# Soft-MoE attention on one core: the order of the last weight steps, and the cut of the output into stores

## The chip, the cores and the metric

One core of a Trainium2 chip runs the whole program. The metric is the device time of one execution in microseconds; the median of 3 runs is 369.21 us (368.94 to 369.48). Engines: PE (TensorE), DVE (VectorE), ACT (ScalarE), POOL (GpSimd) and SP (SyncE), which issues all the transfers that matter here, on one queue.

## The reference

An attention with sigmoid in place of softmax (8 batches, 12 heads, 448 rows, 64 columns) gives x of 3584 x 768. A soft mixture of 8 experts with 4 slots each follows:

```python
logits = x @ phi                                   # 3584 x 32
d = softmax of logits over the 3584 rows;  slot_input = d.T @ x
for e in range(8):                                 # w1: 768 x 1024, w2: 1024 x 768, float32
    slot_out[e] = np.maximum(slot_input[e] @ w1[e], 0.0) @ w2[e]
c = softmax of logits over the 32 slots
return c @ slot_out                                # 3584 x 768, 11 MB
```

## The kernel before

The first stage (to about 285 us) computes attention, logits and slot inputs, and loads the first weights beside it. Then come the w1 steps, and then w2 in two halves of 384 columns: for each half 16 steps n = 2e + g, where step n does experts e = n // 2 and half g of its 1024 hidden rows. A step (`w2_step`, matmul on L804) is four chunks `fl` on four column groups of PE, each float32 matmul two instructions, so 8 in the profile. POOL's copy on L800 puts the expert's 4 slots into `hw[e % 2]` once for each e and half.

Weights come in units of 384 KB; a step takes two. The loads go through SP's queue in the order of use (`load`, L169), as buffers come free; the last two of those are the halves of one load into `wpe`, for steps 13 and 14 of the second half. Step 15's weights are apart: unit `units[N_SEQ + 1]` (chunks 2 and 3) is put into `lt` by `load_kept`; of unit `units[N_SEQ]` the left half (chunk 0) lies in `wk`, loaded early by `load_wk`, and the right half (chunk 1, 192 KB) is loaded into `wpx` by `load_rest` (L137), which runs when no other load is left.

The output has 28 row blocks of 128 rows. `out_tile` (L750, L751) is one matmul of combine weights with the slot outputs of a half (`sts[hf]`) and a copy out of PSUM, on ACT for even and on DVE for odd tiles. Three kinds of stores take the tiles: `out_half` (L757) two row blocks of one half of the columns, 384 KB in pieces of 1536 bytes; `out_rows` (L764) one whole row block, 384 KB in pieces of 3072 bytes; `out_many` (L771) n whole row blocks, in pieces of n times 3072 bytes.

While the second half's steps run, `out_half` stores the first half's columns of row blocks 0 to `NH` - 1, a pair after each of the steps n = 4, 5, and so on. After step 15 the sum is gathered (`gather`, L777, ACT) and spread (`spread_sum`: two matmuls on L788, ACT on L790, DVE on L791), then the whole-row stores go out (`NR` = 2 of one block, then `MANY`), and at the end the second half's columns of blocks 0 to `NH` - 1. The order on PE, ACT, DVE and SP is that of the program.

Of the kernel before, what the change touches and what calls it, by code (L numbers as in the profile page):

```python
# [17 lines left out]
DM, NSLOT, E, SPE, F = 768, 32, 8, 4, 1024  # L18
# [34 lines left out]
FW = (NFC + 1) * NSLOT  # L53
ROWS = 128
NG = B * S // ROWS
NH = 16
LAG_T = 3
C4W = NBK * 4 * NSLOT
NR = 2
MANY = (2, 4, 4)  # L60
GROUPS = ((0, 1), (2, 3), (4, 5), (6,), (7,))
NB2 = 2 * NBK - 1
MANUAL = {mybir.EngineType.PE, mybir.EngineType.SP, mybir.EngineType.DVE, mybir.EngineType.Activation}
# [3 lines left out]
def soft_moe_attention(ctx: ExitStack, tc: tile.TileContext, qk, v, vl, phi, w, wq, w8, wz, cst, out):  # L67
# [71 lines left out]
    def w2_chunk(hf, e, g, fl):  # L139
        k = ("w2", hf, e, g, fl // 2)  # L140
        if k == units[N_SEQ] and fl % 2 == 0:
            return state["wh"]
        return utile[k][:, fl % 2 * HALF:(fl % 2 + 1) * HALF]
# [518 lines left out]
    def av_tile(name):  # L662
        turn[name] += 1
        return ps_av.tile([P, 512], F32, name=f"{name}{turn[name] % 2}")
# [53 lines left out]
    def combine_split(n):  # L718
        lt, k = pieces[n][:2]
        c4 = wc_last[:, n % 3 * C4W:(n % 3 + 1) * C4W].rearrange("p (k a z s) -> p k a z s", k=NBK, a=2, z=2)  # L720
        nc.vector.tensor_copy(c4[:, 0:k, 0, 0, :], lt)
        nc.vector.tensor_tensor(
            out=c4[:, 0:k, 0, 1, :], in0=lt, in1=c4[:, 0:k, 0, 0, :].bitcast(F32), op=ALU.subtract)
        nc.scalar.copy(c4[:, 0:k, 1, :, :], c4[:, 0:k, 0, :, :].bitcast(F32))
        return c4

    def combine_turn(n, c4):
        pt = pt_tile()
        _, k, t0, nt = pieces[n]
        for c in range(k):  # L730
            w = min(P, nt - c * P)
            nc.tensor.transpose(
                out=pt[:, c * P:c * P + w], in_=c4[0:w, c].rearrange("p a z s -> p (a z s)").bitcast(F32),
                identity=csb[0:w, 0:w])
        at0 = t0
        while at0 < t0 + nt:
            i, m = divmod(at0, UNIT)
            w = min(UNIT - m, t0 + nt - at0)
            if m == 0:
                cts[i] = state["wpb"].tile([P, UNIT], F32R, name=f"wc{i + 1}")[:]  # L740
            nc.scalar.copy(cts[i][:, m:m + w], pt[:, at0 - t0:at0 - t0 + w])
            at0 += w
# [10 lines left out]
    def out_half(m, hf):  # L753
        ov = ring_tile().rearrange("p (j c) -> p j c", j=2)
        for j in range(2):
            out_tile(ov[:, j, :], m + j, hf, j)
        nc.sync.dma_start(  # L757
            out[m * ROWS:(m + 2) * ROWS, hf * HALF:(hf + 1) * HALF].rearrange("(j p) c -> p j c", p=P), ov)

    def out_rows(m):  # L760
        ov = ring_tile().rearrange("p (j c) -> p j c", j=2)
        for hf in range(2):
            out_tile(ov[:, hf, :], m, hf, hf)
        nc.sync.dma_start(out[m * ROWS:(m + 1) * ROWS, :].rearrange("p (j c) -> p j c", j=2), ov)  # L764

    def out_many(m, n):
        ov = ring_tile(n)
        for k in range(2 * n):
            t, hf = divmod(k, 2)
            out_tile(ov[:, k * HALF:(k + 1) * HALF], m, hf, hf, t, n)  # L770
        nc.sync.dma_start(out[m * ROWS:(m + n) * ROWS, :].rearrange("(p t) c -> p (t c)", t=n), ov)  # L771
# [3 lines left out]
    def gather(po):  # L775
        so = sb2.tile([P, HALF], F32, name="tmp")
        nc.scalar.copy(so[:], po[:, 0:HALF])  # L777
        return so

    def spread_sum(so, cuts=(0, HALF)):  # L780
        if sts:
            st = wc_last[:, 0:HALF]
        else:
            st = sb2.tile([P, HALF], F32R, name="st")[:]
        parts = list(zip(cuts, cuts[1:]))
        prs = [ps_t.tile([P, 512], F32, name="pt") if k else av_tile("av1") for k in range(len(parts))]
        for pr, (c0, c1) in zip(prs, parts):
            nc.tensor.matmul(pr[:, 0:c1 - c0], rep, so[:, c0:c1], start=True, stop=True)  # L788
        for pr, (c0, c1) in zip(prs, parts):
            (nc.scalar.copy if len(parts) > 1 else nc.vector.tensor_copy)(st[:, c0:c1], pr[:, 0:c1 - c0])  # L790
            nc.vector.tensor_tensor(  # L791
                out=st[64:128, c0:c1], in0=pr[64:128, 0:c1 - c0], in1=st[64:128, c0:c1].bitcast(F32), op=ALU.subtract)
        sts.append(st)

    def w2_step(po, hf, n):
        e, g = divmod(n, 2)
        h = hw[e % 2]
        if g == 0:
            o = NSLOT - SPE
            nc.gpsimd.tensor_copy(  # L800
                h[:, o:o + NFC * NSLOT].rearrange("p (f s) -> p f s", f=NFC)[:, :, 0:SPE], hc[:, e])
        for fl in range(4):
            k = (4 * g + fl) * NSLOT + NSLOT - SPE - SPE * e
            nc.tensor.matmul(  # L804
                po[32 * fl:32 * fl + 32, 0:HALF], h[:, k:k + NSLOT], w2_chunk(hf, e, g, fl),
                start=(n == 0), stop=(n == 2 * E - 1))

    prev = None
    for e in range(E):
# [9 lines left out]

    po = av_tile("av1")  # L820
    for e in range(E):
        w2_step(po, 0, 2 * e)
        w2_step(po, 0, 2 * e + 1)
        if e >= LAG_T:
            combine_turn(e - LAG_T, c4s[e - LAG_T])
        c4s[e] = combine_split(e)
    assert state["next"] == N_SEQ
    so = gather(po)
    po = av_tile("av1")
    for n in range(2 * E):  # L830
        w2_step(po, 1, n)
        if n == 1:
            spread_sum(so)
        if n < LAG_T:
            combine_turn(E - LAG_T + n, c4s[E - LAG_T + n])
            if n == LAG_T - 1:
                sctx.close()
                ps_t = ctx.enter_context(tc.tile_pool(name="ps_t", bufs=4, space=PSUM, reuse_waits="tile"))
        if 4 <= n < 4 + NH // 2:
            out_half(2 * (n - 4), 0)  # L840
    spread_sum(gather(po), (0, HALF // 2, HALF))
    for m in range(NH, NH + NR):
        out_rows(m)
    m = NH + NR
    for n in MANY:
        out_many(m, n)
        m += n
    assert m == NG
    for m in range(0, NH, 2):
        out_half(m, 1)  # L850
# [50 lines left out]
```

## Time and profile before

| | |
|---|---|
| median of 3 runs | 369.21 us (368.94 to 369.48) |
| the profiled execution | 369.13 us, of which the span of instructions is 367.4 us |
| mean granted clock | 0.982 |
| PE busy | 347.7 us (95%) |
| DVE, ACT, POOL busy | 242.4, 222.5, 9.1 us |
| read from and written to memory | 83.53 MB, 11.01 MB |

Shares of busy time are means over stages with different limits: PE is at 9 tenths or more in nearly all slices up to 280 us, while the DMA engines are at 9 tenths or more in the last quarter. Times below are us from the start of the span.

### The profile page before, as it was taken

The numbers are of one execution on the slowest core, as the hardware profiler recorded it, in microseconds if no ns is written. First come the engines' busy times: TensorE is split into PE (matmuls) and PEld (weight loads), VectorE is DVE, ScalarE is ACT, GpSimd is POOL, SyncE is SP. The second block draws the span as 40 slices with busy tenths as digits, with TensorE's granted clock in tenths as the row PEclk, the third lists the DMA queues.
The fourth block names the chain that finished last, engine by engine and source line by source line (L and its number), as shares of the span: only waits on it lengthen the run. The fifth ranks groups of instructions, "written<-read, shape, count | busy, mean of one in ns | idle before, by whom it ended". The sixth has DMA issues, their size and how long they took to land.

```text
span 367.4 us, 10340 instructions
## 1 busy us (share of the span) xinstructions
PE 347.7 (95%) x4309; PEld 159.6 (43%) x4309; DVE 242.4 (66%) x621; ACT 222.5 (61%) x306; POOL 9.1 (2%) x39
## 2 busy tenths in 40 slices
PE   9999999999999999999999999999999999799850
PEld 5333333544444346444434644464556553233620
DVE  0148829887795886959948696889875785123650
ACT  5777777667777773777777387748674114322640
POOL 1000000000000000000000000000003001000000
PEclk9999999999999999999999999999999999989995
DMA  6666675565676663666676377829899999999998
GB/s 218 218 208 205 204 222 186 183 204 163 231 222 211 199 198 114 210 199 202 204 227 184 128 249 251 290 62 366 286 308 363 435 421 430 416 423 405 403 417 300
DMA packets 34639, 95.21 MB, mean 259 GB/s; under 512 B 3616, under 2 KB 17568, under 8 KB 33312
## 3 DMA queue, kind: packets, MB, share of 16 engines
q1 hardware_dynamic: 34592, 94.55, 73.3%
q8 instruction: 34, 0.56, 0.6%
q14 instruction: 13, 0.11, 0.1%
HBM read 83.53 MB, written 11.01 MB: 257 GB/s over the span
## 4 chain that ended last, share of the span: by engine, by line
PE 81%; DMA 14%; DVE 1%; ACT 0%; issue 0%; ACTq 0%; SPq 0%
PE sc L274 35%; PE av L315 34%; DMA wpe<-in_wq_dram 9%; DMA wa<-in_w_dram 5%; PE sc L431 2%; PE sc L377 2%; PE av L187 2%; DVE wa L751 1%; PE av L750 1%; PE sc L359 1%; PE av L545 1%; PE av L290 1%; PE pt L750 1%; PE av L431 0%; PE av L804 0%
## 5 line engine op out<-in xcount | busy, mean ns | idle before, releaser
L282 ACT ACTIVATE att<-sc,sm 128x896 f32<-128x896 f32 x167 | 167.9, 1008 | 81.0 <-PE sc L274 77.8
L315 PE MATMUL av<-att,v 64*64 64x448 f32 x1128 | 131.1, 536 | 0.0
L274 PE MATMUL sc<-qk 64*64 64x448 f32 x896 | 111.7, 537 | 0.0
L315 PEld LDWEIGHTS av<-att,v 64*64 64x64 f32 x1128 | 42.5, 133 | 63.4 <-issue 63.0
L274 PE MATMUL sc<-wk 64*64 64x448 f32 x440 | 59.7, 551 | 0.0
L340 DVE STREAM_TRANSPOSE wa<-wpe 32x384 f32<-32x384 f32 (+5 forms) x144 | 58.0, 403 | 2.2
L274 PEld LDWEIGHTS sc<-qk 64*64 64x64 f32 x896 | 35.6, 133 | 49.7 <-issue 40.4
L340 DVE STREAM_TRANSPOSE wa<-xy 32x192 f32<-32x192 f32 (+3 forms) x96 | 33.1, 344 | 1.6
L322 DVE TENSOR_TENSOR wpe<-wpe,av 128x448 f32<-128x448 f32 x18 | 11.2, 621 | 32.0 <-PE av L315 20.8
L274 PEld LDWEIGHTS sc<-wk 64*64 64x64 f32 x440 | 18.4, 136 | 24.1 <-issue 20.5
L340 DVE STREAM_TRANSPOSE wa<-wpx 32x288 f32<-32x288 f32 (+1 forms) x48 | 24.9, 520 | 0.8
L804 PE MATMUL av<-wa,hw 128*32 128x384 f32 x208 | 20.9, 507 | 2.5 <-DMA wa<-in_w_dram 2.5
L322 DVE TENSOR_TENSOR wpx<-wpx,av 128x448 f32<-128x448 f32 x15 | 9.3, 621 | 19.7 <-PE av L315 17.4
L315 PE MATMUL av<-att,vl 64*64 64x448 f32 x188 | 22.3, 536 | 0.0
L187 PE MATMUL av<-wa,phi 128*32 128x256 f32 x312 | 17.6, 380 | 0.4 <-DVE phi L512 0.4
L322 DVE TENSOR_TENSOR xy<-xy,av 128x448 f32<-128x448 f32 x14 | 8.7, 621 | 8.0 <-ACT xy L318 4.0
L751 DVE COPY wa<-pt 128x384 f32<-128x384 f32 x23 | 11.9, 555 | 3.2 <-PE pt L750 2.8
L751 ACT COPY wa<-av 128x384 f32<-128x384 f32 x23 | 10.7, 481 | 4.6 <-PE av L750 4.0
L187 PEld LDWEIGHTS av<-wa,phi 128*32 128x32 f32 x312 | 9.7, 110 | 7.1 <-DVE tmp L694 0.9
L697 ACT COPY t<-tmp 128x32 f32<-128x32 f32 x8 | 1.7, 218 | 17.5 <-DVE tmp L695 17.5
L315 PEld LDWEIGHTS av<-att,vl 64*64 64x64 f32 x188 | 7.3, 133 | 10.8 <-issue 10.8
L340 DVE STREAM_TRANSPOSE wpe<-xy 32x256 f32<-32x256 f32 (+3 forms) x32 | 11.0, 344 | 0.5
(184 smaller groups left out, 285.6 us busy)
## 6 DMA issues: line engine op xcount, KB each, us to landing
wa<-in_w_dram SPq DMA_DIRECT2D x52, 384.0 KB, 4.1
qk<-in_qk_dram SPq DMA_DIRECT2D x32, 448.0 KB, 3.7
wa<-in_w_dram SPq DMA_DIRECT2D x4, 3072.0 KB, 19.4
v<-in_v_dram SPq DMA_DIRECT2D x48, 192.0 KB, 2.6
wk<-in_qk_dram SPq DMA_DIRECT2D x15, 448.0 KB, 3.4
wa<-in_wq_dram SPq DMA_DIRECT2D x4, 1536.0 KB, 32.5
out_dram<-wa SPq DMA_DIRECT2D x13, 384.0 KB, 7.4
out_dram<-wa SPq DMA_DIRECT2D x2, 1536.0 KB, 7.5
```

Of the source, the lines that this page charges most:

```text
L187: nc.tensor.matmul(ph[32 * j:32 * j + 32, 0:256], phi_sb[:, kc, :], wt, start=(kc == 0), stop=(kc == NKC - 1))
L274: nc.tensor.matmul(sc[h][64 * t:64 * t + 64, 0:S], qkts[pt][r, S + k0:S + k0 + 64], qkts[pt][r, 0:S], start=True, stop=True)
L282: nc.scalar.activation(att[:], tile2[:, :, 0:S], AF.Sigmoid, bias=nbias, scale=QSCALE)
L290: nc.tensor.matmul(o[k][r, 0:t.stop - t.start], w[:, r], att[:, h, t], start=start, stop=stop)
L315: nc.tensor.matmul(o[t][r, 0:S], w, att[row, h, :], start=start, stop=stop)
L322: nc.vector.tensor_tensor(out=x_of(p), in0=x_of(p), in1=av[0][:, 0:S], op=ALU.add)
L340: nc.vector.transpose(y[32 * g:32 * g + 32, k0:k0 + n, c0:c0 + m, BLK * a:BLK * a + BLK], src)
L377: nc.tensor.matmul(lg[32 * j:32 * j + 32, BLK * c0[j]:BLK * (c0[j] + n)], phi_sb[:, hp, :], blocks(x, j if x is xa else (j + 2) % 4, n), s ...
L431: nc.tensor.matmul(sls[t][32 * a:32 * a + 32, :], zt[:, c * BLK:(c + 1) * BLK], y_of(t, gi, c)[:, :, BLK * a:BLK * a + BLK], start=(c == 0 ...
L750: nc.tensor.matmul(pf[:, 0:HALF], ct_of(m, t, n), sts[hf], start=True, stop=True)
L751: (nc.scalar.copy, nc.vector.tensor_copy)[k % 2](ov, pf[:, 0:HALF])
L804: nc.tensor.matmul(po[32 * fl:32 * fl + 32, 0:HALF], h[:, k:k + NSLOT], w2_chunk(hf, e, g, fl), start=(n == 0), stop=(n == 2 * E - 1))
```

## The change

Three edits. Step 15 of the second half moves ahead of steps 13 and 14 (`ORDER2`); the first and last matmul of the sum are told by position, and the copy into `hw` is made when the pair (half, e) changes. `NH` is 14: seven stores by halves in each half, the last of the first half after n = 10. The whole rows are 14 blocks, stored by 1, 1, 2, 4, 2, 4.

```diff
-NH = 16
+NH = 14
-MANY = (2, 4, 4)
+MANY = (2, 4, 2, 4)
+ORDER2 = tuple(range(13)) + (15, 13, 14)
...
+    held_e = {}
+
-    def w2_step(po, hf, n):
+    def w2_step(po, hf, n, first, last):
         e, g = divmod(n, 2)
         h = hw[e % 2]
-        if g == 0:
+        if held_e.get(e % 2) != (hf, e):
+            held_e[e % 2] = hf, e
             o = NSLOT - SPE
             nc.gpsimd.tensor_copy(
...
-                start=(n == 0), stop=(n == 2 * E - 1))
+                start=first, stop=last)
...
-        w2_step(po, 0, 2 * e)
-        w2_step(po, 0, 2 * e + 1)
+        w2_step(po, 0, 2 * e, e == 0, False)
+        w2_step(po, 0, 2 * e + 1, False, e == E - 1)
...
-        w2_step(po, 1, n)
+        w2_step(po, 1, ORDER2[n], n == 0, n == 2 * E - 1)
```

PE around the last steps of the second half, before, right behind step 11 (`wa`: step 12, `wpe`: 13 and 14, `wk`, `wpx`, `lt`: 15; `hw_3401` is for e = 6, `hw_3402` for e = 7; a wait in brackets names a semaphore; DMAHW2, 3 and 4 are those of the two `wpe` loads and of `load_rest`):

```order
L750 MATMUL av_3980<-st,wc_3825 128x384 [waits Activation_49]
L750 MATMUL pt<-st,wc_3825 128x384 [waits DVE_49]
L804 MATMUL av_3849<-wa_3653,hw_3401 32x384 [waits Pool_49]
L804 MATMUL av_3849<-wa_3653,hw_3401 32x384 x3
L804 MATMUL av_3849<-wpe,hw_3401 32x384 [waits DMAHW2_49]
L804 MATMUL av_3849<-wpe,hw_3401 32x384 x3
L804 MATMUL av_3849<-wpe,hw_3402 32x384 [waits DMAHW3_49,Pool_49]
L804 MATMUL av_3849<-wpe,hw_3402 32x384 x3
L804 MATMUL av_3849<-wk,hw_3402 32x384
L804 MATMUL av_3849<-wpx,hw_3402 32x384 [waits DMAHW4_49]
L804 MATMUL av_3849<-lt,hw_3402 32x384 x2
L788 MATMUL av_4007<-tmp,rep 128x192 [waits Activation_49]
```

and with the change:

```order
L808 MATMUL av_3849<-wa_3653,hw_3401 32x384 [waits Pool_49]
L808 MATMUL av_3849<-wa_3653,hw_3401 32x384 x3
L808 MATMUL av_3849<-wk,hw_3402 32x384 [waits Pool_49]
L808 MATMUL av_3849<-wpx,hw_3402 32x384 [waits DMAHW4_49]
L808 MATMUL av_3849<-lt,hw_3402 32x384 x2
L808 MATMUL av_3849<-wpe,hw_3401 32x384 [waits DMAHW2_49]
L808 MATMUL av_3849<-wpe,hw_3401 32x384 x3
L808 MATMUL av_3849<-wpe,hw_3402 32x384 [waits DMAHW3_49]
L808 MATMUL av_3849<-wpe,hw_3402 32x384 x3
L789 MATMUL av_4000<-tmp,rep 128x192 [waits Activation_49]
```

The two output matmuls after step 11 are gone from here, and step 15, with the wait for `load_rest`, stands ahead of steps 13 and 14.

SP's stores before, from the sixth store by halves to the first of the last ones by halves (`load_rest` is the row ahead of the first store, the last load, in both orders):

```order
L757 DMA out_dram<-wa_3956 128x2x384 [waits DMAHW2_49,DVE_49,Activation_49]
L757 DMA out_dram<-wa_3956 128x2x384 [waits DMAHW3_49,DVE_49,Activation_49]
L757 DMA out_dram<-wa_3956 128x2x384 [waits DMAHW4_49,DVE_49,Activation_49]
L764 DMA out_dram<-wa_3956 128x768 [waits DMAHW5_49,DVE_49,Activation_49]
L764 DMA out_dram<-wa_4022 128x768 [waits DMAHW6_49,DVE_49,Activation_49]
L771 DMA out_dram<-wa_4022 128x1536 [waits DMAHW7_49,DVE_49,Activation_49]
L771 DMA out_dram<-wa_4022 128x3072 [waits DMAHW0_49,DVE_49,Activation_49]
L771 DMA out_dram<-wa_4068 128x3072 [waits DMAHW1_49,DVE_49,Activation_49]
L757 DMA out_dram<-wa_4068 128x2x384 [waits DMAHW2_49,DVE_49,Activation_49]
```

and with the change:

```order
L758 DMA out_dram<-wa_3956 128x2x384 [waits DMAHW2_49,DVE_49,Activation_49]
L758 DMA out_dram<-wa_3956 128x2x384 [waits DMAHW3_49,DVE_49,Activation_49]
L765 DMA out_dram<-wa_3956 128x768 [waits DMAHW4_49,DVE_49,Activation_49]
L765 DMA out_dram<-wa_3956 128x768 [waits DMAHW5_49,DVE_49,Activation_49]
L772 DMA out_dram<-wa_4022 128x1536 [waits DMAHW6_49,DVE_49,Activation_49]
L772 DMA out_dram<-wa_4022 128x3072 [waits DMAHW7_49,DVE_49,Activation_49]
L772 DMA out_dram<-wa_4022 128x1536 [waits DMAHW0_49,DVE_49,Activation_49]
L772 DMA out_dram<-wa_4074 128x3072 [waits DMAHW1_49,DVE_49,Activation_49]
L758 DMA out_dram<-wa_4074 128x2x384 [waits DMAHW2_49,DVE_49,Activation_49]
```

One store by halves fewer stands ahead of the whole rows (the first five, ahead of these rows, are alike in both), and a store of two blocks more stands among them; of the last stores by halves there are seven, not eight.

## Rows read from the trace of the kernel before

**Rows 1.** The page, its second part: the mean busy share of the 16 DMA engines in 40 equal slices of the span, in tenths (9 is 90% or more).
```profile
DMA  6666675565676663666676377829899999999998
```

**Rows 2.** Busy time of each engine in four stretches of the end. Columns: stretch, its length, busy time of PE, PE weight load, DVE, ACT and POOL with the number of instructions, granted clock as a share of full speed, mean share of the DMA engines (packets overlap a little, so it can pass 1), GB/s.
```profile
325.00:335.00 10.00, 10.00 (x84) 3.59 (x80) 3.33 (x6) 3.41 (x7) 0.84 (x4) 1.00 1.00 418
335.00:345.00 10.00, 7.86 (x61) 3.89 (x58) 3.15 (x8) 3.46 (x9) 0.21 (x1) 1.00 1.04 398
345.00:355.00 10.00, 8.60 (x32) 6.36 (x32) 8.87 (x18) 7.74 (x17) 0.00 (x0) 1.00 1.04 426
355.00:365.00 10.00, 0.00 (x0) 0.00 (x0) 0.00 (x0) 0.00 (x0) 0.00 (x0) 0.64 1.02 384
```

**Rows 3.** The chain of waits that ended last, in order of time, three of its pieces: start and length in us, what.
```profile
306.08 33.12 DMA wpe<-in_wq_dram
...
339.33 1.53 PE av L804 x16
...
340.94 0.49 ACT tmp L777
```

**Rows 4.** SP's queue in order of time, issues of transfers: start and length of the issue in us, line, transfer. In this order: `load_rest`, the seventh and the eighth store by halves, the first store of one whole row block, the store of two, the first of four, the first store by halves after them, and the last.
```profile
313.39 0.33 SPq L137 DMA_DIRECT2D wpx<-in_wz_dram  x1
339.27 0.37 SPq L757 DMA_DIRECT2D out_dram<-wa  x1
339.77 0.49 SPq L757 DMA_DIRECT2D out_dram<-wa  x1
344.29 0.34 SPq L764 DMA_DIRECT2D out_dram<-wa  x1
345.69 0.87 SPq L771 DMA_DIRECT2D out_dram<-wa  x1
347.99 0.33 SPq L771 DMA_DIRECT2D out_dram<-wa  x1
350.73 1.14 SPq L757 DMA_DIRECT2D out_dram<-wa  x1
360.04 1.25 SPq L757 DMA_DIRECT2D out_dram<-wa  x1
```

**Rows 5.** DMA issues, one at a time: size in KB and the time in us from the start of the issue to its landing. The same transfers as in rows 4, with the second store of one row block (issued at 344.76) behind the first.
```profile
wpx<-in_wz_dram SPq DMA_DIRECT2D x1, 192.0 KB, 26.3
out_dram<-wa SPq DMA_DIRECT2D x1, 384.0 KB, 7.2
out_dram<-wa SPq DMA_DIRECT2D x1, 384.0 KB, 7.7
out_dram<-wa SPq DMA_DIRECT2D x1, 384.0 KB, 4.1
out_dram<-wa SPq DMA_DIRECT2D x1, 384.0 KB, 4.6
out_dram<-wa SPq DMA_DIRECT2D x1, 768.0 KB, 5.5
out_dram<-wa SPq DMA_DIRECT2D x1, 1536.0 KB, 6.8
out_dram<-wa SPq DMA_DIRECT2D x1, 384.0 KB, 8.7
out_dram<-wa SPq DMA_DIRECT2D x1, 384.0 KB, 6.3
```

**Rows 6.** PE in order of time around the last steps: start and length in us, line, operation, tiles, shapes, count, and in brackets idle time of the engine and what ended it. Line 804 is `w2_step`; the rows are steps 11 and 12 (`wa`), 13 and 14 (`wpe`), and of step 15 the first instruction on `wk` and the last two on `lt`.
```profile
335.69 0.85 PE L804 MATMUL av<-wa,hw 128*32 128x384 f32 x8
...
337.01 0.85 PE L804 MATMUL av<-wa,hw 128*32 128x384 f32 x8
337.68 0.83 PE L804 MATMUL av<-wpe,hw 128*32 128x384 f32 x8
339.33 0.85 PE L804 MATMUL av<-wpe,hw 128*32 128x384 f32 x8 [0.82 <-DMA wpe<-in_wq_dram]
339.97 0.48 PE L804 MATMUL av<-wk,hw 128*32 128x384 f32 x1
...
340.33 0.49 PE L804 MATMUL av<-lt,hw 128*32 128x384 f32 x2
```

**Rows 7.** POOL in order of time, the copy into `hw` for e = 7.
```profile
336.70 0.21 POOL L800 COPY hw<-t 128x32 f32<-128x32 f32 x1 [2.44 <-PE av L804]
```

**Rows 8.** PE in order of time around the pause at 318 us, columns as in rows 6.
```profile
317.59 0.55 PE L732 MATMUL sc<-csb,wc 128*128 128x128 f32 x3
320.69 1.51 PE L804 MATMUL av<-wa,hw 128*32 128x384 f32 x8 [2.55 <-DMA wa<-in_w_dram]
```

**Rows 9.** Busy time of each engine in stretches around that pause, columns as in rows 2.
```profile
314.00:318.10 4.10, 4.10 (x42) 1.61 (x34) 1.28 (x5) 1.89 (x5) 0.42 (x2) 1.00 0.99 425
318.10:320.30 2.20, 0.04 (x1) 0.00 (x0) 0.05 (x1) 1.16 (x3) 0.00 (x0) 1.00 0.99 413
320.30:323.80 3.50, 3.11 (x12) 1.16 (x13) 0.00 (x0) 0.00 (x0) 0.21 (x1) 0.51 1.01 425
```

**Rows 10.** Time from issue to landing of loads in the first stage, by line: 44 loads of `v` (192 KB), 21 of `vl` (64 KB), 33 of weights (384 KB).
```profile
DMA to landing us min/median/max: 2.2/2.6/4.8
DMA to landing us min/median/max: 1.7/2.0/5.7
DMA to landing us min/median/max: 3.2/4.0/4.8
```

## The prediction

> **What bounds the kernel now.** I went from the end backwards. The page's line of DMA activity stands at 9 tenths in every slice of the last quarter, up to the last [rows 1], and the table of stretches gives the 16 engines a share of 0.99 to 1.04 from 325 to 365 us at 384 to 426 GB/s, while PE, DVE and ACT stop at 355 [rows 2]. So the tail is a queue of transfers that never runs empty: its end is bytes over rate, and a change counts only if it alters that rate or lets the queue run dry. The chain of waits says what feeds it: the second half of the last weight load (issued 306.08, landing 33.12 us later, 339.2), 16 matmul instructions of `w2_step` in 1.53 us, then ACT's `gather` at 340.94 [rows 3], the spread, and the first store of a whole row block at 344.29 [rows 4].
>
> Between 339.77 and 344.29 SP issues no store [rows 4]. The queue lives on eight half stores issued before: adding each issue time to its time to landing [rows 4, 5], the seventh lands at 346.5, the eighth at 347.5, and the first whole-row store at 348.4, right behind. The second lands at 349.4, the two-block store at 351.2, the first four-block store at 354.8, the first half store of the end at 359.4 and the last at 366.3. No gap anywhere. From these: a half store costs (366.3 - 359.4)/7 = 0.99 us of queue, a two-block store 1.8 (351.2 - 349.4), a four-block store 3.6.
>
> **The change, part by part.** *Step 15 ahead of 13 and 14.* The step is said to be of kept weights. Three of its four chunks are (`wk`, and `lt` twice). The fourth, `wpx`, is the 192 KB that `load_rest` fetches, and that is the last load in the queue: issued at 313.39, landing 26.3 us later, at 339.7 [rows 4, 5], 0.5 us behind the second half of the last `wpe` load. The order of the changed kernel puts that matmul, with its wait, in front of all eight matmuls of steps 13 and 14, and PE takes them as they stand. So PE, which before used the pause for step 13 (at 337.68, [rows 6]), now stands still until 339.7 and then has three steps to do, not one and a part.
>
> In numbers: before, the landing at 339.2 released a matmul at 339.33, 0.14 us later, and the next step followed 0.64 us on (339.33 to 339.97, [rows 6]); the last instruction ends at 340.33 + 0.49 = 340.82. After: 339.70 + 0.14 = 339.84, two steps of 0.64, and a last step of 0.85 (its row's length): 341.97. `gather`, the spread and the first whole-row store follow as before, all 1.15 us later: 344.29 + 1.15 = 345.44. POOL's copy of `hw` for e = 7 is needed one step sooner; it still waits for step 11, whose matmuls stand at 335.69 as before, so it ends near 336.9 [rows 7], and the `wk` matmul of step 15 would start no earlier than 337.0 anyway. No DMA is issued by the moved step.
>
> *14 row blocks by halves, not 16.* The half store after step 11 goes, with its two matmuls and two copies; they lay beside other work and come back later in a whole-row store. What it takes from the queue is the cover: the last thing queued is now the seventh half store, landing at 346.5, and the first whole-row store is not issued before 345.44.
>
> What does a store cost that meets an empty queue? None in this trace does. The nearest rows are lone loads on the same queue in the first stage: 192 KB of `v` land after 2.2 us at the least, 64 KB of `vl` after 1.7, and 384 KB of weights after 3.2 at the least and 4.0 in the middle [rows 10]. Brought to 384 KB at 0.99 us for 384 KB, they give 2.2 + 0.5 = 2.7; 1.7 + 0.8 = 2.5; and 3.2. I take 2.7: `v` is nearest in kind, alone on the queue; the weights are issued right behind another load. So the first whole-row store lands at 345.44 + 2.7 = 348.1, not behind the seventh half store at 346.5 + 1.0 = 347.5. Against 348.4 before that is 0.3 us sooner, but with one half store fewer done.
>
> The Trainium skill (DMA: Bandwidth & Descriptors, the section Anatomy of one DMA) gives a fit of about 2.0 us fixed plus the bytes at 436 GB/s, measured on another issuing path than this kernel's. For 384 KB that is an estimate of 2.9 us, and the sum below would be 0.2 us larger; no run here shows such a store.
>
> *Stores of 1, 1, 2, 4, 2, 4.* Behind the first whole-row store the queue has one two-block store more (1.8) and then one half store fewer (the first half's left before it, the second half's is one of the seven, not eight: 0.99). That is +0.8 us against before. Supply behind it: the four-block store was issued 3.70 us after the first (347.99 - 344.29, [rows 4]); with the queue fed from empty, its two single blocks and two-block store last 1.0 + 1.0 + 1.8 = 3.8 us, so it arrives just in time; a tenth more may be lost there, none later.
>
> Sum with the clock as it is: -0.3 + 0.8 = **+0.5 us**, with a tenth for that seam +0.6; from +0.3 (2.5 us) to +1.1 (3.2 us and the seam). The bytes are the same throughout; packets of two blocks in place of halves are worth 2 x 0.99 - 1.8 = 0.2 us, already inside.
>
> *The pause itself.* PE ends step 12 and the `wk` matmul at about 337.5 to 337.8 (step 11 from 335.69, step 12 right behind it with no store's matmuls between, `wk` at 337.0) and starts again at 339.84: 2.0 to 2.3 us still. The trace has one pause of that length: PE ended at 318.14 and resumed at 320.69, 2.55 us, and the granted clock was 1.00 until 320.3 and 0.51 over the 3.5 us that follow, the lower of its levels, 1.2 GHz; a step that takes 0.85 us took 1.51 there [rows 8, 9]. The pause of 0.82 us at 338.5 cost nothing [rows 6]. The new pause is nearer the first, so I take it that the clock falls. If it falls as PE resumes, 3.4 us at half speed do 1.7 us of the 2.13 us of steps: +1.7. If it falls a microsecond later, the remaining 1.13 us double, and part of the spread too: about +1.4. I take +1.5, which moves the first whole-row store to 346.9, with the queue empty meanwhile, so all of it counts.
>
> The Trainium skill (TensorE: Matmul & The Clock Gate, Part 1) says that the point at which the clock changes differs between runs of the same kernel. One profiled execution cannot show that; it is why the next case is given nearly as much chance.
>
> Forecast: the profiled execution took 369.13 us (span 367.4), 0.08 below the median 369.21. 369.13 + 0.6 + 1.5 = **371.2 us**. Its own bounds are +0.3 + 1.4 and +1.1 + 1.7: 370.8 to 371.9.
>
> **The rivals.** *The clock holds* through the pause: +0.6, 369.7 us, from 369.4 to 370.2. For it: the new pause is shorter than the one that cost the clock. Against: by little.
>
> *The last load is in time* (not slower). If step 15's fourth chunk has landed before the first half of the `wpe` load (337.3, some 2.4 us sooner than in the trace), only step 14 is left after 339.2: the matmuls end at 339.33 + 0.85 = 340.18, 0.64 sooner; the first whole-row store is issued at 343.65, before the seventh half store lands, and lands behind it at 347.5. That is -0.9 + 0.8 = -0.1: 369.0 us. It turns once the first whole-row store lands by 347.6, so is issued by 344.9; with 0.6 us of steps to spare that needs the load at about 339.1. Against it: issue and queue before 339 are untouched, and `wpx` stands last among the loads in both orders.
>
> *Larger stores are cheaper than the rows say*, enough to win: it takes 0.8 us over the sum; the rows have 0.2 us for the blocks moved. Little speaks for it.
>
> *That the change doesn't do what it says*: the order of the changed kernel has the moved step, the seven half stores and the six whole-row ones, so no.
>
> **How the numbers follow.** A measurement of this kernel can tell 0.2%, 0.74 us. Clock falls 0.47, slower throughout. Clock holds 0.41; its +0.6 lies close under 0.74 and its interval on both sides: 0.18 slower, 0.23 the same. Load in time 0.10, of which 0.08 the same and 0.02 faster; cheaper stores 0.02, faster. Together faster 0.04, the same 0.31, slower 0.65. The range goes from 369.5, the lower part of the second case, to 371.9, the upper bound of the first; outside are the last two cases and the edges, under 0.2.
>
> **What would show it.** In the profile after: PE with a pause of 2 us or more before the `wpx` matmul of step 15, released by the `wz` load at about 339.7; all of steps 13 and 14 behind it; `gather` at 342.1, or at 343.3 to 343.8 with the clock at half in the slices around 341; the first whole-row store issued at 345.4, or 346.9; a notch in the DMA share between 345 and 348, where before there is none; the end 0.6 or 2.1 us later. I am wrong if step 15 does not wait, if the DMA share stays at 1.0 through 348, or if the last stores land as early as before with the notch there.

## The result and the profile after

The changed kernel takes 370.97 us (median of 13; 369.78 to 372.79) against 369.21 before: 1.0058 of the time, interval 1.0044 to 1.0071, slower (the ratio is estimated from all executions; the two medians alone give 1.0048). Two more sets of it, below, gave 1.0037 (1.0023 to 1.0052) and 1.0065 (1.0042 to 1.0089). The profiled execution took 370.83 us, with a span of 369.0.

The chain of waits of the changed kernel, in order of time, now runs through `load_rest` where [rows 3] had the `wpe` load:

```profile
313.85 26.36 DMA wpx<-in_wz_dram
...
340.25 2.17 PE av L808 x22
...
342.50 0.49 ACT tmp L778
```

PE in order of time at that place, where [rows 6] shows it before (idle time and its releaser in brackets):

```profile
336.21 1.50 PE L808 MATMUL av<-wa,hw 128*32 128x384 f32 x16
337.53 0.81 PE L808 MATMUL av<-wk,hw 128*32 128x384 f32 x2
340.25 0.51 PE L808 MATMUL av<-wpx,hw 128*32 128x384 f32 x1 [1.92 <-DMA wpx<-in_wz_dram]
...
340.62 1.77 PE L808 MATMUL av<-wpe,hw 128*32 128x384 f32 x15
```

PE stands still for 1.92 us ahead of step 15's chunk on `wpx`, until the load lands at 340.21; the rest of step 15 and two whole steps follow in 2.17 us. `gather` comes at 342.50, 2.29 us behind that landing; before it came 1.24 us behind it (340.94 and 339.7). Then the first whole-row store, the first and the last store by halves of the end (issue on SP, and size and time to landing):

```profile
345.85 0.34 SPq L765 DMA_DIRECT2D out_dram<-wa  x1
out_dram<-wa SPq DMA_DIRECT2D x1, 384.0 KB, 2.7
353.32 1.16 SPq L758 DMA_DIRECT2D out_dram<-wa  x1
out_dram<-wa SPq DMA_DIRECT2D x1, 384.0 KB, 8.4
361.35 1.23 SPq L758 DMA_DIRECT2D out_dram<-wa  x1
out_dram<-wa SPq DMA_DIRECT2D x1, 384.0 KB, 6.7
```

and the DMA engines in 40 slices of 344 to 347.5, share in tenths and GB/s:

```profile
DMA  9999987664655434344932311000004799798999
GB/s 404 404 351 386 351 334 298 246 246 176 228 193 193 158 140 158 140 158 158 293 140 88 123 35 70 35 18 35 18 18 176 281 456 386 281 492 351 421 351 421
```

The queue dies away from 344.4 on, is all but empty from 346.2 to 346.6 (shares under a tenth), and full again at 346.8: the notch that [rows 2] does not have. The clock held through this pause and to the end of PE's work (table of stretches, columns as in [rows 2]):

```profile
337.40:340.20 2.80, 0.94 (x6) 0.15 (x2) 0.00 (x0) 0.00 (x0) 0.04 (x1) 1.00 1.04 392
340.20:343.00 2.80, 2.14 (x22) 0.66 (x22) 0.00 (x0) 0.48 (x1) 0.00 (x0) 1.00 1.07 400
343.00:346.00 3.00, 2.29 (x11) 1.68 (x11) 1.45 (x4) 1.61 (x5) 0.00 (x0) 1.00 0.78 289
345.00:346.60 1.60, 1.55 (x8) 1.18 (x8) 1.37 (x3) 1.04 (x3) 0.00 (x0) 1.00 0.32 113
361.00:363.00 2.00, 0.00 (x0) 0.00 (x0) 0.00 (x0) 0.00 (x0) 0.00 (x0) 0.50 1.03 364
363.00:365.00 2.00, 0.00 (x0) 0.00 (x0) 0.00 (x0) 0.00 (x0) 0.00 (x0) 0.50 1.04 368
```

### The profile page after: what moved, and what is told of

It reads as the page before. It is cut to its first block, busy times and chain, and to the rows that moved or that the text cites. A ratio compares the mean times of both kernels' runs of the same rounds, so it can differ in the third digit from the quotient of the medians.

```text
span 369.0 us, 10337 instructions
## 1 busy us (share of the span) xinstructions
PE 348.4 (94%) x4309; PEld 159.9 (43%) x4309; DVE 242.3 (66%) x621; ACT 222.3 (60%) x306; POOL 9.0 (2%) x39
## 4 chain that ended last, share of the span: by engine, by line
PE 81%; DMA 13%; DVE 1%; ACT 0%; issue 0%; DVEq 0%; ACTq 0%; SPq 0%
PE sc L275 35%; PE av L316 34%; DMA wpx<-in_wz_dram 7%; DMA wa<-in_w_dram 6%; PE av L188 3%; PE sc L432 2%; PE sc L378 2%; PE av L751 1%; DVE wa L752 1%; PE sc L360 1%; PE av L546 1%; PE pt L751 1%; PE av L291 1%; PE av L808 1%; PE av L432 0%; PE av L354 0%
## 6 DMA issues: line engine op xcount, KB each, us to landing
wa<-in_w_dram SPq DMA_DIRECT2D x4, 3072.0 KB, 19.5
```

## The experiments

Medians of each set, and ratios to the kernel before on the same chip, estimated from all executions of both (so not quite the quotients of medians):

| run | us | ratio (95%) |
|---|---|---|
| e1_stores_only | 369.32 | 1.0006 (0.9997 to 1.0015) |
| e2_order_only | 369.92 | 1.0026 (1.0017 to 1.0035) |
| e3_rest_first | 369.84 | 1.0025 (1.0013 to 1.0037) |
| e7_cover_18 | 369.38 | 1.0007 (0.9995 to 1.0018) |
| e4_warm | 370.26 | 1.0034 (1.0022 to 1.0046) |
| e5_nh12 | 370.22 | 1.0031 (1.0020 to 1.0042) |
| e8_rest_first_16 | 369.30 | 0.9999 (0.9990 to 1.0008) |
| e6_change_again | 370.51 | 1.0037 (1.0023 to 1.0052) |
| e9_long_pause | 370.85 | 1.0057 (1.0036 to 1.0078) |
| e10_fine_cut | 369.56 | 1.0005 (0.9994 to 1.0017) |
| e11_change_third | 371.80 | 1.0065 (1.0042 to 1.0089) |

**The cut of the stores alone** (e1; the change with `ORDER2` in the old order):

```diff
-ORDER2 = tuple(range(13)) + (15, 13, 14)
+ORDER2 = tuple(range(13)) + (13, 14, 15)
```

> The change's cut of the stores (14 row blocks by halves; whole rows in 1, 1, 2, 4, 2, 4) with the steps in the order of before. Theory A, the late matmuls and the empty queue: the first whole-row store is issued about as before, 15 us after the first store by halves, the seventh half store is hardly done then, the queue stays nearly full, and the time is that of before less 0.1 us, 369.0 to 369.3. Theory B, the new cut is slow in itself (in the changed kernel 19.6 us pass from the landing of the first whole-row store to the last landing, where 18.8 were worked out): these 19.6 us appear here too, and the time is 369.7 to 370.0. Theory C, the clock after the long pause: no long pause here, 369.0 to 369.3.

369.32, no difference that shows. By the time A and C are right (0.02 us above their range) and B falls; but the trace bears out the first half of B. Its first whole-row store, and its first and last store by halves of the end:

```profile
344.18 0.34 SPq L765 DMA_DIRECT2D out_dram<-wa  x1
out_dram<-wa SPq DMA_DIRECT2D x1, 384.0 KB, 3.1
351.63 1.17 SPq L758 DMA_DIRECT2D out_dram<-wa  x1
out_dram<-wa SPq DMA_DIRECT2D x1, 384.0 KB, 8.6
359.66 1.24 SPq L758 DMA_DIRECT2D out_dram<-wa  x1
out_dram<-wa SPq DMA_DIRECT2D x1, 384.0 KB, 6.9
```

From the landing of the first (347.3) to the last landing (366.6) pass 19.3 us, nearly the 19.5 of the changed kernel, and the stores by halves of the end land (366.56 - 360.23)/6 = 1.06 us apart. That costs no time that shows, as the first whole-row store lands 1.1 us sooner than in the kernel before.

**The order alone** (e2; `NH` = 16, `MANY` = (2, 4, 4)):

> The change's order of steps (15 before 13 and 14) with the stores of before (16 row blocks by halves). The pause of some 2 us before step 15's chunk in wpx and the delay of the first whole-row store by 1.15 us must be there. Theory A: the eighth half store covers most of the delay, so 369.2 to 369.6. Theory B: the cut is that of before, so 369.2. Theory C: where the clock falls in the pause, the first whole-row store is another 1.5 us later and the eighth half store no longer covers it: the runs split, some at 369.3 and some at 370.4 to 370.8.

369.92: the order alone costs 0.26%, more than A had for it, with no split. The eighth half store does not cover the delay on all engines: in its trace the DMA share is 0.83 and 0.92 in the two stretches around the first whole-row store.

```profile
345.00:347.00 2.00, 1.95 (x8) 1.50 (x7) 2.00 (x5) 1.67 (x5) 0.00 (x0) 1.00 0.83 306
347.00:349.00 2.00, 2.00 (x8) 1.82 (x8) 1.83 (x5) 1.80 (x4) 0.00 (x0) 1.00 0.92 367
```

**The load in time** (e3), and the same with the stores of before (e8: `NH` = 16, `MANY` = (2, 4, 4)):

```diff
             cut = size // 2 if n + size == N_SEQ else size
+            if n + size == N_SEQ:
+                load_rest()
...
-        if state["next"] < N_SEQ:
+        if state["call"] < len(REFILL) - 1 or e == E - 1:
             refill()
-        else:
-            load_rest()
```

> The changed kernel with the 192 KB of load_rest issued ahead of the two halves of the wpe load, not behind them, so that step 15's weights are all there when its turn comes. Theory A: no pause before step 15, only step 14 is left after the last landing (which comes 0.5 us later, as it is now a wpe half), the first whole-row store is issued 0.1 us sooner than in before and 1.3 sooner than in the change; the queue stays nearly full: 369.0 to 369.3. Theory B: 369.7 to 370.0, the new cut being slow. Theory C: no long pause, 369.0 to 369.3.

> The change's order of steps with load_rest's 192 KB ahead of the wpe halves, and the stores of before (16 row blocks by halves): no pause, one step left after the last landing, first whole-row store at 344.2 or a little sooner, and eight half stores for cover. Theory A with D: the queue is never empty, the engines stay out of step, the last half stores take 0.98 us: the time of before, 368.9 to 369.2, not better, as the end is bytes over rate. Rival (the order itself costs): 369.5 or more.

e8 is the kernel before to 0.1% (0.9999): with its weights there, step 15 ahead of 13 and 14 costs nothing, and gains nothing either, though only one step is left behind the last landing. With 14 blocks by halves (e3) the loss shrinks from 0.58% to 0.25% and does not vanish: A expected 369.0 to 369.3, and 369.84 lies in B's range; from the first whole-row landing to the last pass 19.5 us in its trace (347.6 to 367.1), B's stretch. Its queue still has a thin spot, a share of 0.86 in 345 to 347, where e8 has 1.05:

```profile
345.00:347.00 2.00, 2.00 (x8) 1.82 (x8) 1.91 (x5) 1.77 (x4) 0.00 (x0) 1.00 0.86 330
```

```profile
345.00:347.00 2.00, 2.00 (x9) 1.81 (x8) 1.92 (x5) 1.71 (x4) 0.00 (x0) 1.00 1.05 394
```

**More cover** (e7; the change with `NH` = 18, `MANY` = (2, 2, 4)):

> The change's order of steps with 18 row blocks by halves (whole rows in 1, 1, 2, 2, 4): the wait for load_rest and the late first whole-row store stay, but nine half stores are queued ahead of it. Theory A: the queue never runs empty, the last landing comes as in before plus 0.2 us for two more blocks by halves: 369.3 to 369.6, though the first whole-row store is issued 1.15 us late. Theory B (the order costs nothing, the cut of 1, 1, 2, 4, 2, 4 does): 369.4 as well, so this run cannot tell A from B alone. Theory C: with a fallen clock the first whole-row store lands at most 0.2 us late, so no split of the runs over 0.5 us.

369.38, 1.0007: within its interval the cost of the order is gone. The trace is of the slowest of its eleven executions (370.68) and does not have the pause: the steps ahead came later there, PE reached step 15 only as `load_rest` landed at 340.9, and the late first whole-row store comes mostly from that. It was issued at 346.53, 2.2 us later than in the kernel before:

```profile
340.72 0.51 PE L808 MATMUL av<-wk,hw 128*32 128x384 f32 x1
340.93 0.51 PE L808 MATMUL av<-wpx,hw 128*32 128x384 f32 x1
346.53 0.34 SPq L765 DMA_DIRECT2D out_dram<-wa  x1
out_dram<-wa SPq DMA_DIRECT2D x1, 384.0 KB, 4.1
```

It landed at 350.6, right behind the ninth half store (349.6), so the queue covered a store as late as that; the end of that trace is 1.4 us later than before, of which the landing of `load_rest` has 1.2. With e8 this puts the cost of the order on the wait for the load and on a queue too short to cover it. What 18 blocks by halves do in the old order was not run.

**An empty queue without the order** (e5; the kernel before with `NH` = 12, `MANY` = (2, 2, 4, 2, 4)):

> The kernel before, its steps in the old order, with 12 row blocks by halves in place of 16 (whole rows in 1, 1, 2, 2, 4, 2, 4), so that the queue runs empty without any late matmul: the sixth half store lands at 345.5, the first whole-row store is issued at 344.3 and lands at 347.0 instead of 348.4. Theory D (DMA engines that start together after an empty queue stay in step, and then a half store takes 1.06 us and not 0.98): the last six half stores take 1.05 to 1.07 us each and the engines end within 0.4 us of each other; the last landing comes 0.9 us later than before: 369.8 to 370.2. Rival (the slower half stores of the change have to do with PE's pause or with its cut of the stores): 0.98 us each, 369.4 to 369.6.

370.22, 0.94 us over the kernel before on its chip, as D expected (0.9; the time itself lies 0.02 us above D's range). The queue ran short as meant: the DMA share is 0.48 from 343 to 345 us. First and last store by halves of the end, in e5 and in e8 (issue; time to landing):

```profile
352.98 1.18 SPq L757 DMA_DIRECT2D out_dram<-wa  x1
out_dram<-wa SPq DMA_DIRECT2D x1, 384.0 KB, 9.3
359.66 1.24 SPq L757 DMA_DIRECT2D out_dram<-wa  x1
out_dram<-wa SPq DMA_DIRECT2D x1, 384.0 KB, 8.0
```

```profile
350.97 1.14 SPq L758 DMA_DIRECT2D out_dram<-wa  x1
out_dram<-wa SPq DMA_DIRECT2D x1, 384.0 KB, 8.9
360.25 1.23 SPq L758 DMA_DIRECT2D out_dram<-wa  x1
out_dram<-wa SPq DMA_DIRECT2D x1, 384.0 KB, 6.5
```

Behind the first one's landing, five stores take from 362.3 to 367.7 in e5, 1.06 to 1.09 each by the rounding; in e8 seven take from 359.9 to 366.8, 0.98 each, as in [rows 4, 5]. The last three us of the DMA engines in 40 slices, e5 and then e8, show what differs:

```profile
DMA  9999999999999999999998300000000000000000
```

```profile
DMA  9999999999998544432232100000000000000000
```

In e5 all 16 engines end together, within two slices; in e8 they drop out one by one over 0.9 us. An empty queue is not needed for that: in e1 the queue thinned to a share of 0.89 from 343 to 345 and no lower in the next stretches, and its engines end nearly together too, in 40 slices of 364.3 to 367.3:

```profile
DMA  9999999999999999999999632000000000000000
```

So D holds in what was measured, not in its condition: as far as these traces go, engines come level where the queue runs dry on the foremost of them, and then the last landings of stores by halves are 1.06 us apart. That being level makes 1536-byte pieces slower is not shown.

**The clock** (e4, and the change again, e6):

```diff
     for n in range(2 * E):
+        if n == 13:
+            pd = av_tile("av0")
+            for _ in range(7):
+                nc.tensor.matmul(pd[:, 0:P], ident, ident, start=True, stop=True)
         w2_step(po, 1, ORDER2[n], n == 0, n == 2 * E - 1)
```

> The changed kernel with seven 128 x 128 matmuls of the identity with itself, into a free PSUM bank, between steps 12 and 15, so that PE stands still for a few tenths of a us before the load_rest chunk and not for 2. Theory C (the clock falls in the pause in some executions, and costs about 1.5 us there): the spread to 372.8 us that the changed kernel showed goes, all runs lie below 371.6, and the median is 0.1 to 0.4 us lower than that of the changed kernel on this chip. Rival (the slow runs of the change come from something else, such as the start of the program or the DMA queue): the spread stays and the median is the same.

> The changed kernel as it is, on the same chip as the three others, for a second trace and a second set of times: median 370.6 to 371.2 with one to four of some twelve runs over 372 us. Theory C wants these runs here and none of them with the matmuls that fill the pause.

370.26 and 370.51, and nothing over 371.4 in either: no separation, and none of the executions over 372 us that e6 was to have. The added matmuls also ran until 340.3 in e4's trace, 0.5 us past the landing of `load_rest`. So the pause was made longer (e9, the change with the chunk on `wk` behind the others), beside a third set of the change (e11):

```diff
-        for fl in range(4):
+        for fl in ((1, 2, 3, 0) if (hf, n) == (1, 15) else range(4)):
```

> The changed kernel with the chunks of step 15 in the order 1, 2, 3, 0, so that its matmul on wpx comes first and nothing is left to do in the pause: about 2.5 us still instead of 1.9, as long as the pause at 318 us that cost the clock in the kernel before. Theory C (a pause of this length costs the clock, and the clock costs 1.5 us): in most executions the granted clock falls to 0.5 near 338 to 342 us, the first whole-row store is issued 1 to 1.5 us later than in the changed kernel, and the median is 371.5 to 372.3. Rival (no fall, or one that costs nothing): the first whole-row store comes 0.2 us later at most, the median is that of the change, 370.5 to 371.0.

> The changed kernel as it is, beside the two others on one chip: median 370.5 to 371.0. If some executions lie over 372 us as three of the first thirteen did, while the kernel with the longer pause has most of its executions there, they are theory C's; if the longer pause changes nothing, they are not.

e9: 370.85, the median of its rival, with three of ten at 372.4 to 373.5, not most: the longer pause gives no more slow executions than the change has (below). In its profiled execution PE stood still for 2.91 us and the clock held:

```profile
338.00:340.00 2.00, 0.00 (x0) 0.00 (x0) 0.00 (x0) 0.00 (x0) 0.00 (x0) 1.00 1.04 392
340.00:342.00 2.00, 1.54 (x20) 0.81 (x24) 0.00 (x0) 0.00 (x0) 0.00 (x0) 1.00 1.07 400
```

e11 had three of six at 372.4 to 372.8, which puts its median (371.80) over the 370.5 to 371.0 expected. Its profiled execution is one of them (372.39), and there the clock fell, behind a pause of 1.97 us:

```profile
339.89 0.51 PE L808 MATMUL av<-wpx,hw 128*32 128x384 f32 x1 [1.97 <-DMA wpx<-in_wz_dram]
...
340.26 2.71 PE L808 MATMUL av<-wpe,hw 128*32 128x384 f32 x15
347.40 0.34 SPq L765 DMA_DIRECT2D out_dram<-wa  x1
```

```profile
341.00:343.00 2.00, 1.97 (x14) 0.23 (x5) 0.00 (x0) 0.00 (x0) 0.00 (x0) 0.50 1.06 397
343.00:345.00 2.00, 1.40 (x5) 1.40 (x5) 0.00 (x0) 0.80 (x2) 0.00 (x0) 0.50 0.92 346
345.00:347.00 2.00, 1.51 (x5) 1.01 (x5) 0.94 (x3) 0.80 (x2) 0.00 (x0) 0.50 0.17 63
347.00:349.00 2.00, 2.00 (x9) 1.61 (x8) 1.89 (x4) 1.52 (x4) 0.00 (x0) 0.81 0.42 154
```

The granted clock is 0.50, the lower level of 1.2 GHz, from 341 to past 347; the last steps take 2.71 us where they took 1.77 with the clock held, and the first whole-row store comes 7.55 us behind the landing of `load_rest` (339.85), not 5.64. The DMA engines are nearly idle through 345 to 347, share 0.17. Of the 24 executions of the change in three sets, six lie at 372.3 to 372.8 and the others at 369.8 to 371.5, with medians 372.5 and 370.75. Only one of the six was traced. Their mean granted clocks do not settle the others: 0.973 or 0.974 in four of the six but 0.982 in two, against 0.974 to 0.988 in the eighteen. And one of the twelve executions of e3, which has no pause ahead of step 15, took 371.59, also 1.75 us over its median. That the fallen clock makes the slow group is shown for one execution and likely for the rest.

**A finer last load** (e10; e3 with the last load in three):

```diff
+            cuts = (0, 2, 3, 4) if n + size == N_SEQ else (0, size)
+            for a, b in zip(cuts, cuts[1:]):
```

> The changed order and cut of stores with load_rest ahead of the wpe loads, and the last wpe load cut in three (step 13's two units, then step 14's one by one), so that half a step is left after the last landing: the first whole-row store 0.3 us sooner against the last landing than with two halves. Theory A with D: if that keeps the queue from running empty ahead of it, the engines stay out of step and the time is 369.0 to 369.2, no better than before by more than 0.1 us, as the end is bytes over rate; if not, the last half stores take 1.05 us and the time is 369.3 to 369.8, as with 14 blocks before.

369.56, 1.0005: no difference to before that shows, with the 14 blocks of the change, and nothing won. That is in the range for a queue that still runs short (369.3 to 369.8), though the last stores by halves of its trace land 1.0 us apart, not 1.05. No version beats the kernel before.

## Why the prediction was right

**The wait on the last load: right.** The `wpx` chunk waits for `load_rest`, PE pauses, and `gather` is 1.05 us later against that landing (predicted 1.15). e8 shows the other side: with the load in time the order is free.

**The empty queue: right.** The first whole-row store landed 2.7 us after its issue (345.85 to 348.55), the value taken from `v`'s loads. With nine half stores as cover (e7) and with PE in time (e1) the cost vanishes, and an empty queue without the order costs 0.31% (e5). The Trainium skill's fit (DMA: Bandwidth & Descriptors, Anatomy of one DMA), made on another issuing path, was an estimate of 2.9 us; the trace has 2.7, and 2.9 in e5.

**The stores behind it: mis-sized.** The sum had +0.8 us from the landing of the first whole-row store to the end. It is 19.5 us (348.55 to 368.05) where before it was 17.9 (348.4 to 366.3): +1.6. A half store was taken at 0.99 us; here it takes (368.05 - 361.7)/6 = 1.06. Seven of them are 0.5 us; the whole-row stores and rounding are the rest. More than half of the excess is in e1 too (19.3 us there), whose queue did not run empty.

The term went wrong by reading one landing for each store, the last. The trace records 16, one for each DMA engine. In the kernel before, from the first store by halves of the end to the last, the earliest landing moves from 357.96 to 365.45, 1.07 us a store, and the latest from 359.47 to 366.36, 0.98. So 0.99 was the pace of an engine that lagged, 1.5 us behind the foremost at first and 0.9 at last; the foremost took 1.07 all along. The same holds of the cover: the seventh half store of the change lands between 344.62 and 346.96, so the foremost engine ran dry 2.3 us ahead of the last, by which the cover was counted. Where the engines come level, no lag is left to make up. So "the clock holds" is not +0.6 but about +1.2 in the trace, and +1.5 by medians (370.75 against 369.2).

**The clock: right in kind, wrong in weight.** I gave the case nearly half and took it as likeliest. Six of 24 executions lie 1.75 us over the others, where 1.5 was taken; the one traced has the fall (at half for some 6.8 us, where 3.4 was taken). Reading the length of the pause against the one in [rows 8] was the failing step: 1.97 us cost the clock in one execution, 1.92 did not in another of the same kernel, nor did 2.91 in e9. The pause of [rows 8] itself is no rule. PE stands still at 318 us in all thirteen traces of these kernels, for 2.3 to 2.7 us; the clock fell there or up to 1.3 us behind in ten of them and held in three (e1, e2, e5). In e1, where [rows 9] has 0.51:

```profile
320.55 0.85 PE L808 MATMUL av<-wa,hw 128*32 128x384 f32 x8 [2.45 <-DMA wa<-in_w_dram]
320.30:323.80 3.50, 3.25 (x25) 1.45 (x25) 1.12 (x2) 0.59 (x2) 0.21 (x1) 1.00 1.00 421
```

That the point of change differs between runs of one kernel is what the Trainium skill says (TensorE: Matmul & The Clock Gate, Part 1), of the rise under matmuls. These traces agree for the fall: where it came, it began between 319.9 and 322.3 us.

So that 371.2 came so near to 370.97 is in part luck. Both cases were put about a microsecond too low: with the clock held the sum said 369.4 to 370.2 and those executions have a median of 370.75; with the clock fallen it said 370.8 to 371.9 and the slow six have 372.5. The forecast added a term too small by 0.6 to 0.9 us and a fall of 1.5 us that about a quarter of the executions show, and the two errors nearly cancelled. Part of the profiled execution's +1.7 us, 0.5, is the first stage: `load_rest` landed at 340.2, not 339.7; other traces of these kernels have it between 339.6 and 340.9, so that is not the change.

What stays open: e3 lies 0.2% above e1 and e10, though its thinnest stretch has a share of 0.86 and theirs 0.89 (343 to 345 in both). The intervals overlap by a little; if the difference is real, its cause was not settled. So what 14 blocks by halves cost with the first whole-row store in time is known only as 0.05 to 0.25%, and the upper end is what B wanted.

## What to carry to other kernels

Before a step is moved forward because its operands are kept, look up the landing of each operand: one late piece of 192 KB held two whole steps in the engine's order. Where the end is a queue of transfers, count its cover in us ahead of the next producer, on the earliest engine to run dry and not on the last landing, and do not take the distance of two last landings for the price of a transfer while engines lag; taking cover away and delaying the producer cost little each alone (0.06% and 0.26%) and 0.37 to 0.65% together. A pause of PE is a chance of a clock loss, not a threshold to be read from one trace: of thirteen traces with the same pause ten had the loss.

## What the runs showed of the hardware

The DMA engines of one queue can be a us out of step, as e8's end shows, and more: the eighth half store of the kernel before lands on one engine at 345.17 and on another at 347.43. After a queue that ran empty (the change, e5) or thin (e1) they end nearly together, and stores in pieces of 1536 bytes then run at 364 to 368 GB/s (the changed kernel's rows of 361 to 365 above), where the kernel before has 381:

```profile
361.00:363.00 2.00, 0.00 (x0) 0.00 (x0) 0.00 (x0) 0.00 (x0) 0.00 (x0) 0.50 1.04 381
```

The granted clock of PE fell at pauses of 2.0 us (e11) and 2.3 to 2.7 us (at 318 us, ten traces), and held through pauses of 1.9 us (the change), 2.5 and 2.7 us (e1 and e5, at 318 us) and 2.9 us (e9).
